# Six prefetch hints and six branches in TensorE's program of a cached attention decode kernel

## The chip, the cores and the metric

The kernel runs on one core of one Trainium2 chip. The metric is the device time of one execution in microseconds (us). Three runs of the kernel before gave 1265.35 to 1266.34 us, with a median of 1266.06 us. Differences of about 0.2% (2.5 us) are taken as what a measurement of this kernel can tell from no change.

Five engines work side by side, each with its own program: TensorE (PE in the profile, with its weight loads as PEld), VectorE (DVE), ScalarE (ACT), GpSimd (POOL) and SyncE (SP). SP issues nearly all the transfers from device memory. Engines wait for each other through semaphores.

## The reference

What is computed is one decode step: a gated sum of an attention block over a long cache and a small token-mixing MLP.

```python
Hq, Hkv, Sk, Dh = 16, 8, 65536, 256            # D = 448, one token
q = (x @ wq).reshape(1, 1, 16, 256)            # two query heads share one KV head
scores = einsum("bhqd,bhkd->bhqk", q, k) * Dh**-0.5
o = einsum("bhqk,bhkd->bhqd", softmax(scores), v)
a = o.reshape(1, 1, 4096) @ wo
b = token_mlp(layernorm(x))                    # w1, b1, gelu, w2, b2 over a token axis of length 1
g = sigmoid((x * gate_w).sum(-1))
return g * a + (1 - g) * b
```

The K cache and the V cache hold 8 x 65536 x 256 bf16 numbers each, 268 MB apiece. All of it has to be read once.

## The kernel before, in words

**Tiling.** The cache is cut into `NP` = 32 blocks, four for each of the 8 KV heads. A block is 16384 keys, laid out as 128 partitions by `NV` = 128 key rows of 256 numbers: 8.39 MB of K and 8.39 MB of V. `kring` holds one and a half blocks of K, `vbuf` one block of V.

**TensorE's loop (lines 521 to 562).** It runs 33 times over `j`. Pass `j` does three things in order. First come the maxima of the block before (`maxima`, line 384). Then come the keys of block `j` (`keys`, line 375), in eight groups `k` of 16 key rows: `transposes(k)` (line 333) turns 16 tiles of K by matmuls into `kst` (line 348), and `scores(k - 1)` (line 360) multiplies 32 turned tiles by the query (line 369). Groups 0 to 3 read the half of K that is loaded at row `HV` = 64 and up; groups 4 to 7 read the other half, at one of two places, so they stand twice in the program, in an `If` and an `Else` (lines 355 to 358). Group 4 has three more `If`s ahead of it (lines 338 to 340). Last come the values of the block before (`values`, line 404): eight matmuls for the denominators (line 393) and 128 for the values (line 400), in pieces that the `pieces` list cuts (0 to 72, 72 to 96, 96 to 112, 112 to 128). The first piece stands twice as well, since the last pass reads it from `kring`. The last pass ends with `tail` (line 467).

[...] Ahead of the loop stands a head that runs once: it turns `x`, computes the queries (lines 495 to 499, which signal `s_q`), and clears two accumulators.

**The other engines.** VectorE and ScalarE copy the turned K tiles out of `kst` (lines 656 and 796), VectorE finds the maxima and scales the accumulator by the change of the maximum (lines 662 to 685, which signal `s_acc`), ScalarE makes the exponentials (line 783, which signal `sem_exp`).

**The order of the transfers.** SP runs a written-out order (lines 255 to 314; every load of K and V is recorded at line 263). K of block `j` is issued when TensorE has turned groups 0 to 3 of block `j - 1` (line 286, semaphore `sem_tr`). V of block `j - 1` follows when TensorE has finished the values before it (line 274, semaphore `sem_pv`), since `vbuf` is free only then. All loads go through one queue in this order. Blocks 0 to 3 start up differently: the two halves of K of blocks 2 and 3 are issued as separate transfers into whichever part of `kring` is free. Pass 2 (`j == LEAD`) has no values.

## Time and profile before

| What | Value |
|---|---|
| Median of three runs | 1266.06 us (1265.35 to 1266.34) |
| Span of the profiled execution, first to last instruction | 1264.2 us |
| Median less span (start and end around the profile's instructions) | 1.9 us |
| TensorE matmuls busy | 955.4 us, 76% of the span |
| VectorE busy, ScalarE busy | 497.4 us and 544.5 us, 39% and 43% |
| Bytes moved | 544.37 MB in 12054 packets |

How to read it: no time of the profiled execution is given apart from its span, so sums are made on the span and 1.9 us are added. A row of the timeline has a start, a busy time, an engine, a source line, what was written from what, and how often; in brackets stands the idle time of the engine ahead of it and what ended that. "issue" there means that the profile shows nothing that the engine waited for: its sequencer was busy with branches, registers or the fetch of code. A row of waits has the total, the number of times and the longest. A row of a DMA queue has packets, megabytes and a share of the time of 16 DMA engines. A row of windows has the stretch, then the busy time of each engine with its instruction count, the granted TensorE clock, the DMA share and GB/s; DMA packets are counted by their start there, so shares of short stretches go above 1 and below it in turn.

### The profile page before, as it was taken

To read this page: it belongs to the slowest core of one execution; us is meant where nothing else is said; L and a number is where in the kernel's file an instruction comes from. 1 tells how busy PE (TensorE), PEld (TensorE's weight loads), DVE (VectorE), ACT (ScalarE), POOL (GpSimd) and SP (SyncE) were. 2 spreads that over 40 slices of the span, in tenths; PEclk is the share of its full clock that TensorE was granted. 3 is DMA by queue.
4 is the path that set the end of the run, shared out by engine and by line. 5 is a ranking of instruction groups with operands and counts; after the bars stand their busy time and mean duration, and the time that the engine had idled before them with its cause. 6 is when DMAs were issued, how large, how long until landed. Compare 5 with 4: busy or idle time off the path is not lost.

```text
span 1264.2 us, 39788 instructions
## 1 busy us (share of the span) xinstructions
PE 955.4 (76%) x17107; PEld 879.2 (70%) x17107; DVE 497.4 (39%) x1124; ACT 544.5 (43%) x691; POOL 0.9 (0%) x7
## 2 busy tenths in 40 slices
PE   4778887778776787767877768876769867698786
PEld 3677876668766687666876657875668756687674
DVE  3333434443543444444344423342333423334342
ACT  2444543345533455333554334443344533345451
POOL 0000000000000000000000000000000000000000
PEclk9878887898888897888987889887888878888898
DMA  9999999999999999999999999999999999999998
GB/s 412 434 421 426 441 431 435 433 431 433 435 433 435 433 431 431 431 440 433 431 435 422 435 435 442 433 425 435 431 431 435 435 433 431 435 431 431 427 448 355
DMA packets 12054, 544.37 MB, mean 431 GB/s; under 512 B 1417, under 2 KB 1676, under 8 KB 2956
## 3 DMA queue, kind: packets, MB, share of 16 engines
q1 hardware_dynamic: 11954, 544.22, 99.7%
q8 instruction: 7, 0.11, 0.0%
q10 hardware_dynamic: 90, 0.01, 0.0%
q14 instruction: 3, 0.02, 0.0%
HBM read 544.22 MB, written 0.00 MB: 430 GB/s over the span
## 4 chain that ended last, share of the span: by engine, by line
DMA 63%; PE 34%; issue 1%; DVE 1%; SPq 0%; DVEq 0%; ACT 0%
DMA kring<-in_A_k_cache_dram 60%; PE kst L348 25%; PE sps L369 6%; DMA vbuf<-in_A_v_cache_dram 2%; PE acc L400 2%; DMA wo_sb<-in_A_wo_dram 1%; PE acc L450 0%; PE sps L388 0%; PE prj L461 0%; SPq L263 0%; PE acc L393 0%; DVE ktT L656 0%; ACT z_b L801 0%; PE sps L386 0%; DVE mrow L667 0%
## 5 line engine op out<-in xcount | busy, mean ns | idle before, releaser
L348 PE MATMUL kst<-ident,kring 128*128 128x128 f32 x4096 | 555.4, 296 | 200.3 <-DMA kring<-in_A_k_cache_dram 177.1
L348 PEld LDWEIGHTS kst<-ident,kring 128*128 128x128 f32 x4096 | 504.1, 154 | 209.2 <-issue 204.1
L796 ACT ACTIVATE ktT<-kst 128x1024 bf16<-128x1024 bf16 x512 | 499.3, 1022 | 348.8 <-PE kst L348 348.0
L656 DVE COPY ktT<-kst 128x1024 bf16<-128x1024 bf16 x512 | 353.9, 692 | 444.0 <-PE kst L348 418.5
L369 PEld LDWEIGHTS sps<-qcur,ktT 128*128 128x128 bf16 x8192 | 237.8, 96 | 2.8 <-issue 0.3
L369 PE MATMUL sps<-qcur,ktT 128*128 128x2 bf16 x8192 | 236.6, 163 | 0.0
L400 PE MATMUL acc<-vbuf,pT 128*2 128x256 bf16 x4008 | 155.2, 328 | 7.2 <-DMA vbuf<-in_A_v_cache_dram 3.6
L400 PEld LDWEIGHTS acc<-vbuf,pT 128*2 128x2 bf16 x4008 | 109.2, 100 | 44.9 <-issue 6.2
L779 ACT ACTIVATE fade<-mdif 128x2 f32<-128x2 f32 x32 | 6.5, 204 | 297.1 <-DVE mdif L673 297.1
L667 DVE TENSOR_REDUCE mrow<-sps 2x1 f32<-2x128 f32 x32 | 8.9, 279 | 156.5 <-PE sps L386 156.5
L388 PEld LDWEIGHTS sps<-mdiag,mones 2*128 2x128 f32 x64 | 11.0, 214 | 27.9 <-DVE mdiag L669 27.9
L783 ACT ACTIVATE pT<-sps,mneg 128x64 f32 x128 | 30.3, 334 | 0.0
L386 PE MATMUL sps<-ident,mcol 128*2 128x128 f32 x32 | 8.9, 279 | 27.7 <-issue 26.2
L388 PE MATMUL sps<-mdiag,mones 2*128 2x2 f32 x64 | 13.7, 282 | 21.3 <-DVE mdiag L669 21.3
L801 ACT ACTIVATE z_b<-z_b 128x448 bf16<-128x448 bf16 x14 | 8.1, 577 | 48.2 <-DVE z_b L643 48.2
L393 PE MATMUL acc<-pT,ones_sq 128*128 128x32 bf16 x256 | 11.9, 181 | 21.8 <-issue 18.3
L386 PEld LDWEIGHTS sps<-ident,mcol 128*2 128x2 f32 x32 | 2.6, 80 | 36.4 <-issue 28.1
L690 DVE COPY accs<-acc 128x288 f32<-128x288 f32 x8 | 3.7, 457 | 60.9 <-PE acc L400 60.9
L662 DVE TENSOR_REDUCE mcol<-sps 128x2 f32<-128x256 f32 x32 | 13.5, 423 | 35.5 <-PE sps L369 35.5
L393 PEld LDWEIGHTS acc<-pT,ones_sq 128*128 128x128 bf16 x256 | 8.7, 99 | 25.8 <-issue 22.2
L685 DVE TENSOR_SCALAR acc<-acc,fader 128x256 f32<-128x256 f32 x32 | 15.8, 493 | 2.5
L672 DVE TENSOR_SCALAR mneg<-sps 128x2 f32<-128x2 f32 x32 | 5.1, 160 | 16.7 <-PE sps L388 16.7
(108 smaller groups left out, 174.6 us busy)
## 6 DMA issues: line engine op xcount, KB each, us to landing
kring<-in_A_k_cache_dram SPq DMA_DIRECT2D x8, 4096.0 KB, 23.8
kring<-in_A_v_cache_dram SPq DMA_DIRECT2D x1, 4608.0 KB, 27.1
wo_sb<-in_A_wo_dram SPq DMA_DIRECT2D x7, 448.0 KB, 25.7
vbuf<-in_A_wq_dram SPq DMA_DIRECT2D x1, 3072.0 KB, 10.4
vbuf<-in_A_v_cache_dram SPq DMA_DIRECT2D x1, 1536.0 KB, 9.2
vbuf<-in_A_v_cache_dram SPq DMA_DIRECT2D x1, 1024.0 KB, 11.3
vbuf<-in_A_v_cache_dram SPq DMA_DIRECT2D x1, 768.0 KB, 12.7
vbuf<-in_A_wq_dram SPq DMA_DIRECT2D x1, 512.0 KB, 11.2
```

The lines of the kernel that those rows point to most:

```text
L348: ins = pe.transpose(kst[:, b, i * P:(i + 1) * P], kring_f[:, at + NT * (k % DC) + 4 * b + i, :], ident[:, :])
L369: ins = pe.matmul(sps[:, 0, 2 * (NT * k + nt):2 * (NT * k + nt) + 2], ktT[:, par, b, ntl * DH + dj:(ntl + 1) * DH:2], qcur[:, dj, :], star ...
L386: pe.transpose(mxT, mcol[:, :], ident[:, :]).then_inc(s_mT, 1)
L388: pe.matmul(mxB, mones[:, :], mdiag[:, :], start=True, stop=True).then_inc(s_mB, 1)
L393: pe.matmul(acc[:, DENC:SELC], ones_sq[:, :], pT[:, r, :], start=False, stop=(r == BODY - 1), skip_group_check=True)
L400: ins = pe.matmul(acc[o:o + REP, 0:DH], pT[:, r, 2 * nt:2 * nt + 2], buf[:, n, :], start=False, stop=False, skip_group_check=True)
L656: vec.tensor_copy(ktT[:, k % KTB, b, :], kst_b[:, b, :]).then_inc(sem_ev[b], 1)
L662: vec.tensor_reduce(out=mcol[:, :], in_=scores_all.rearrange("p (n hh) -> p hh n", hh=REP), axis=AX.X, op=ALU.max)
L667: vec.tensor_reduce(out=mrow[:, :], in_=mxT, axis=AX.X, op=ALU.max)
L685: vec.tensor_scalar(acc[:, 0:DENC], acc[:, 0:DENC], fader[:, :], None, op0=ALU.mult).then_inc(s_acc, 1)
L783: ins = act.activation(pT[:, bass.ds(p0, DC), hh:2 * NT:REP], scores_all.rearrange("p (a r n hh) -> p a hh r n", a=2, r=DC, hh=REP)[:, hal ...
L796: act.activation(ktT[:, k % KTB, b, :], kst_b[:, b, :], AF.Copy).then_inc(sem_ev[b], 1)
```

## The change

Six times at the head of TensorE's program, ahead of everything else that it does, the change marks a place for a branch hint. Each place names one of six branches further down. [...]

The six branches are new and stand inside the loop. Each compares a register with 1 << 20, which the register never reaches, and goes to the same label whether it is taken or not; that label is the next instruction. So no branch changes what is computed. They stand at the top of a pass (`hop(0)`), ahead of groups 3 and 6 of the keys (`hop(1)`, `hop(2)`), in `values` after the waits and ahead of the denominators (`hop(3)`), after 32 of the first 72 value matmuls (`hop(4)`), and after the first piece (`hop(5)`). For `hop(4)` the first piece in its `If` half is cut in two calls, which issue the same 72 matmuls in the same order.

```diff
+    NHOP = 6
...
             one = ones_sq[0:1, 0:1]
+            hints = [pe.mark_branch_hint_location() for _ in range(NHOP)]
+
+            def hop(i, reg):
+                name = "hop_%d" % i
+                pe.br_lt(reg, 1 << 20, on_true=name, on_false=name).branch_hint(hints[i])
+                nc.switch_bb(name)
...
                 for k in range(1, BODY):
+                    if k % 3 == 0:
+                        hop(k // 3, c0)
                     transposes(k, c0 + k, j, *where)
...
                 pe.wait_ge(sem_exp, pe.snap(v + 1, min_val=2, max_val=NP + 1))
+                hop(3, j)
                 denominators()
                 with pe.If(j < NP):
                     pe.wait_ge(sem_v, pe.snap(v * 16, min_val=16, max_val=16 * NP))
-                    some(0, NRING, vbuf)
+                    some(0, 2 * NT, vbuf)
+                    hop(4, j)
+                    some(2 * NT, NRING, vbuf)
                 with pe.Else():
                     piece_wait(0)
                     some(0, NRING, kring)
+                hop(5, j)
...
                 g = pe.snap(g_reg, min_val=1, max_val=H + 1)
+                hop(0, j)
                 with pe.If(j > LEAD):
```

The hints run once. `hop(0)` runs in all 33 passes, `hop(1)` and `hop(2)` in the 32 passes that have keys, `hop(3)` and `hop(5)` in the 32 passes that have values, and `hop(4)` in 31 of these, all but the last.

## The prediction

> **What bounds the kernel now.** I read the first page from the top: busy time, transfers, queues, and the chain that ended last.

> ```profile
> span 1264.2 us, 39788 instructions
> PE 955.4 (76%) x17107; PEld 879.2 (70%) x17107; DVE 497.4 (39%) x1124; ACT 544.5 (43%) x691; POOL 0.9 (0%) x7
> ...
> q1 hardware_dynamic: 11954, 544.22, 99.7%
> q8 instruction: 7, 0.11, 0.0%
> ...
> DMA 63%; PE 34%; issue 1%; DVE 1%; SPq 0%; DVEq 0%; ACT 0%
> ```

> No compute engine is busy for more than 76% of the span, and queue q1, which carries the cache, is busy for 99.7% of it. So the time is a volume over a rate, plus what lies at the two ends. The chain gives TensorE 34%, but the chain names the last releaser of each wait; it does not ask whether the queue was still full when the next load came. For that I take the busy time by stretches.

> ```profile
> 0.00:3.00 3.00, 0.43 (x5) 0.29 (x5) 1.55 (x10) 0.00 (x0) 0.90 (x7) 1.00 0.35 99
> 3.00:122.00 119.00, 81.13 (x1400) 73.69 (x1401) 40.33 (x90) 46.31 (x57) 0.00 (x0) 0.87 1.00 431
> 122.00:1259.00 1137.00, 871.45 (x15661) 803.61 (x15658) 454.13 (x1021) 497.88 (x634) 0.00 (x0) 0.86 1.00 433
> 1259.00:1264.20 5.20, 2.41 (x44) 1.64 (x44) 1.43 (x6) 0.35 (x1) 0.00 (x0) 0.76 0.27 99
> ```

> The last two numbers of each row are the DMA share and GB/s. From 122 us on the transfers run at 433 GB/s without a gap. The start-up from 3 to 122 us runs at 431 GB/s: 119 x (1 - 431/433) = 0.55 us were lost there. That is all that a change on TensorE could win in the transfers.

> Next, how much the transfers can bear when TensorE is late: the issues with their time to landing, and TensorE's longest wait.

> ```profile
> vbuf<-in_A_v_cache_dram SPq DMA_DIRECT2D x31, 28.1
> kring<-in_A_k_cache_dram SPq DMA_DIRECT2D x28, 27.8
> ...
> PE kst L348 <- DMA kring<-in_A_k_cache_dram: 177.1, 29, 9.7
> ```

> A block of 8.39 MB takes 8390/433 = 19.4 us, yet lands 27.8 or 28.1 us after its issue. It stood in the queue behind another block for some 8.5 us. The first load shows how long a transfer takes to begin:

> ```profile
> 0.74 0.41 SPq L255 DMA_DIRECT2D wo_sb<-in_A_wo_dram  x1
> ```

> It was issued at 0.74 us, and the share of 0.35 over the first 3 us is 1.05 us of full work, so transfers began near 1.95, about 1.2 us after. That leaves some 7 us: in the middle of the run a load may be issued 7 us later before the queue runs dry. TensorE also waits 177.1/29 = 6.1 us per pass for K. A few tenths more per pass disappear in this.

> There is one place without that cover, in the start-up:

> ```profile
> 65.60 0.33 SPq L263 DMA_DIRECT2D vbuf<-in_A_v_cache_dram  x1
> ...
> 116.72 0.33 SPq L263 DMA_DIRECT2D kring<-in_A_k_cache_dram  x1
> ...
> 72.52 6.01 PE L348 MATMUL kst<-ident,kring 128*128 128x128 f32 x32 [6.95 <-DMA kring<-in_A_k_cache_dram]
> ...
> wo_sb<-in_A_wo_dram SPq DMA_DIRECT2D x7, 448.0 KB, 25.7
> vbuf<-in_A_wq_dram SPq DMA_DIRECT2D x1, 3072.0 KB, 10.4
> ...
> vbuf<-in_A_wq_dram SPq DMA_DIRECT2D x1, 512.0 KB, 11.2
> ```

> The load at 116.72 us is the second half of K of block 3. What was issued ahead of it is 4032 KB = 4.13 MB of weights (one load of each of the three rows) and five and a half blocks of 8.39 MB, together 50.3 MB. At 433 GB/s from 1.95 us these end at 118.1, or 118.7 with the 0.55 us lost. Issue at 116.72 plus 1.2 us is 117.9. Here nothing is to spare: what TensorE loses between 72.52 us, where K of block 1 releases it, and 116.72 us may become time of the whole kernel.

> **The change, part by part.** *The hints at the head.* They stand ahead of everything on TensorE, once. What hides them is a wait for a small load:

> ```profile
> PE acc L486 <- DMA b_b<-in_B_b_dram: 8.7, 1, 8.7
> ```

> Six instructions at 0.23 us, the dearest that I find below for a sequencer instruction, are 1.4 us inside 8.7 us. Without that cover they would still only move the queries, whose signal releases V of block 0, queued behind the weights and K of block 0 until 1.95 + 12.5 MB/433 = 30.9 us. Cost 0.

> *What the hints may fetch.* Queue q8 carries seven packets of 16 KB. The queues by window say when: one up to 19 us, six up to 73 us, and after that one small packet of the other code queue only.

> ```profile
> q8 instruction: 1, 0.02, 0.3%
> ...
> q8 instruction: 6, 0.10, 0.7%
> ...
> q1 hardware_dynamic: 10924, 513.48, 99.7%
> q14 instruction: 1, 0.01, 0.0%
> ...
> 48.51 0.55 PE L348 MATMUL kst<-ident,kring 128*128 128x128 f32 x3 [2.17 <-issue]
> 63.10 2.47 PE L400 MATMUL acc<-vbuf,pT 128*2 128x256 bf16 x51 [3.58 <-issue]
> ```

> I take these for TensorE's code, since they fall in its first pass, where TensorE stops in the middle of a run of equal matmuls, for 2.17 and 3.58 us, with nothing to wait for; in the 31 later passes neither packets nor such stops show. So the loop stays in the engine's instruction memory once it is there. If the hints bring the code in early, 5.75 us of stops go. What is late next is K of block 1: TensorE would end the first pass 5.75 us sooner and wait 12.7 us in place of 6.95. V of block 1 would be issued near 60 in place of 65.60 us, into a queue that is full until 1.95 + 29.3 MB/433 = 69.6 us (the weights and three blocks). Nothing gained. The packets take 0.7% of 16 engines over 54 us, 1.0 us of one engine each; moved before the loads begin, all seven give back 7/16 = 0.4 us, and fetched twice they cost as much. I take 0, with -0.55 (the loss of the start-up) and +0.4 as ends.

> *The branches.* No row shows a single branch. Three places bound one. Between the last value matmul of pass 1 and the first tile of pass 2 lie some six branches and ten register instructions. Ahead of group 4 lie four branches. Groups 5 to 7 have an `If` and an `Else` each, group 2 has none:

> ```profile
> 79.17 1.95 PE L348 MATMUL kst<-ident,kring 128*128 128x128 f32 x16
> 81.76 1.94 PE L348 MATMUL kst<-ident,kring 128*128 128x128 f32 x16
> 85.07 1.96 PE L348 MATMUL kst<-ident,kring 128*128 128x128 f32 x16 [0.59 <-issue]
> 87.77 1.97 PE L348 MATMUL kst<-ident,kring 128*128 128x128 f32 x16
> 90.37 1.95 PE L348 MATMUL kst<-ident,kring 128*128 128x128 f32 x16
> 92.96 1.95 PE L348 MATMUL kst<-ident,kring 128*128 128x128 f32 x16
> 100.80 5.49 PE L400 MATMUL acc<-vbuf,pT 128*2 128x256 bf16 x128
> 107.69 3.83 PE L348 MATMUL kst<-ident,kring 128*128 128x128 f32 x32 [1.40 <-issue]
> ```

> The first: 1.40/6 = 0.23 us each, with the register work put on the branches. The second: 0.59/4 = 0.15 us. The third: groups 5 to 6 and 6 to 7 are 2.60 and 2.59 us apart, groups 1 to 2, without a branch, 2.59. So where matmuls are queued ahead a branch costs nothing, because the sequencer runs ahead of the array; the 128 value matmuls, which have several branches among them, also run in one piece. An exposed branch lies between 0 and 0.23 us; I take 0.15, from the second place, the nearest to bare branches.

> `hop(1)` and `hop(2)` stand like groups 5 to 7, `hop(4)` and `hop(5)` inside the value matmuls: 0. `hop(3)` stands behind the waits for the accumulator and the exponentials, with the denominators queued behind it and nothing running: 0.15. `hop(0)` stands at the top of a pass, with the maxima and the keys behind it: 0.15. From 72.52 to 116.72 us run hops 1 to 5 of pass 1 and hops 0 and 1 of pass 2: 2 x 0.15 = **0.3 us**, with 0 and 7 x 0.23 = 1.6 us as ends. In the later passes the same 0.3 us, at most 6 x 0.23 = 1.4, lie inside the 6.1 us of waiting and the 7 us of queue: 0. At the end, `hop(0)`, `hop(3)` and `hop(5)` of the last pass lie ahead of this wait for the last pieces of V:

> ```profile
> 1258.19 0.61 PE L400 MATMUL acc<-vbuf,pT 128*2 128x256 bf16 x16 [1.62 <-DMA vbuf<-in_A_v_cache_dram]
> ```

> 3 x 0.23 = 0.7 us is less than 1.62: 0.

> [...]

> **Sum.** Span 1264.2 + 0.3 = 1264.5 us; with the 1.9 us around it, 1266.4, against the median of 1266.06. That is 0.03%, far under the 0.2% (2.5 us) that a measurement of this kernel can tell from no change. I forecast no change.

> **The rivals.** *The first pass gains (faster, within 0.2%).* The hints bring the code in before the loads begin. For it speak the two stops; against it, that the wait for K hides them. At most 0.55 us: 1265.5.

> *The loop no longer stays resident (slower).* The six branches make the loop longer. Nothing shows how much more code the engine keeps; seven packets are known to fit. If the longer loop, or lines taken up by hints, push it over that edge, all seven are fetched again in each of 32 passes. TensorE's stops, 5.75 us as in the first pass, would still fit in its 6.1 us of waiting. What can't be hidden is the queue: 7 x 1.0 us of one engine in 16 is 0.44 us per pass, 14 us in all if the packets spread evenly, and up to 1.0 x 32 = 32 us if one engine serves the same packet each time: 1280 to 1298. It decides from the first packet that comes back in every pass, one each costing 2 us spread or 32 on one engine. Against it: a few instructions are little beside 0.11 MB.

> [...]

> *A new stop in the first two passes (slower).* If the hints upset the order in which code comes in, or a branch meets code that is not there yet, one or two stops of 2.17 to 3.58 us fall between 72.52 and 116.72 us, once, and are paid in full: 1268.6 to 1273.6, starting from 1266.4.

> *The change does not do what it says:* the hints fetch nothing and the branches vanish. 1266.1, no different.

> **How the numbers follow.** Forecast 0.71 (1265.2 to 1267.7). First pass gains 0.07. Change without effect 0.05. Loop no longer resident 0.10. New stop 0.07. Faster by over 0.2% would need a gain four times what the start-up lost; I keep 0.02 of the first rival for what I have not seen. So faster 0.02, same 0.05 + 0.05 + 0.71 = 0.81, slower 0.17. The range reaches below to the 0.55 us plus the half microsecond by which the three runs spread, 1264.8, and above to one stop of 2.17 us in the start-up with the same spread, 1269.2.

> **What would show it.** Right: q1 at 99.7%, the stretch from 122 to 1259 us at 433 GB/s, the load of 116.72 us at 116.7 to 117.3, no more packets on q8 after 73 us. The hints at work: no stop near 48 and 63 us, V of block 1 issued near 60. Wrong: packets of q8 in every pass; stops of over 2 us between 72 and 117 us; time to landing under 21 us in the middle of the run, which would mean a queue that runs dry.

## The result, and the profile after

| | before | after |
|---|---|---|
| Median | 1265.93 us (1265.35 to 1266.79) | 1269.61 us (1265.39 to 1275.99) |
| Executions | 16 | 16 |
| Executions above 1268 us | 0 | 10 |
| Ratio after to before | | 1.0025, 95% interval 1.0015 to 1.0035 |

The change made the kernel slower by 0.25% by the ratio of the comparison, or 3.7 us between the medians. That is just over the 0.2% that counts as a difference here. The median lies 0.4 us above the upper end of the prediction's range, 1269.2 us; the ratio, put on the prediction's 1266.06 us, gives 1269.2 us, that end itself. The executions are as telling as the median: those of before lie within 1.4 us, those of after within 10.6 us. Four of after's are as fast as before (1265.39 to 1265.88 us) and ten lie above 1268 us. So this is no fixed price per pass. Something happens in some executions and not in others. The profiled execution of after is its longest, 1275.99 us, so its profile shows the loss enlarged. (The ratios here and below leave out executions over 1.5% above the fastest of their kernel: three of `e10_twice`, one of `e3_hops_fit`; medians and ranges hold them all.)

The first page of after, the lines that answer to those of before:

```profile
span 1274.2 us, 39985 instructions
PE 989.1 (78%) x17107; PEld 904.2 (71%) x17107; DVE 496.6 (39%) x1124; ACT 545.7 (43%) x691; POOL 0.9 (0%) x7
...
q1 hardware_dynamic: 11954, 544.22, 99.3%
q8 instruction: 8, 0.13, 0.0%
...
DMA 48%; PE 43%; issue 3%; DVE 3%; DVEq 1%; ACT 0%; SPq 0%
```

The volume is the same and q1's share fell from 99.7% to 99.3%: the queue ran dry. TensorE is busy 33.7 us longer with the same 17107 matmuls, so they ran slower. VectorE, which the change does not touch, now has 3% of the chain of work that ended last, against 1%.

Where was it lost? The same bytes lie ahead of each landing of a block of K in both kernels, so the time from landing to landing tells. A landing is the start of the key matmuls that waited for it. Three stretches, before and then after: up to K of block 4, from block 5 to block 7, and from block 17 to block 19. The columns are stretch, engines, clock, DMA share, GB/s.

```profile
3.00:169.77 166.77, 119.42 (x2089) 109.47 (x2090) 59.83 (x134) 69.76 (x88) 0.00 (x0) 0.88 1.01 433
208.47:287.02 78.55, 58.87 (x1050) 54.14 (x1051) 35.03 (x83) 35.00 (x45) 0.00 (x0) 0.85 1.00 433
676.33:754.87 78.54, 57.35 (x1051) 53.65 (x1051) 30.88 (x67) 34.02 (x44) 0.00 (x0) 0.85 1.00 433
```

```profile
3.00:173.67 170.67, 119.93 (x2089) 109.58 (x2090) 59.77 (x134) 69.71 (x88) 0.00 (x0) 0.87 1.01 428
212.46:293.47 81.01, 67.13 (x1051) 61.34 (x1051) 33.13 (x77) 34.76 (x44) 0.00 (x0) 0.75 0.97 409
683.22:764.71 81.49, 65.97 (x1050) 60.32 (x1051) 33.32 (x76) 34.76 (x44) 0.00 (x0) 0.77 0.99 417
```

The span grew by 10.0 us. Of these 3.9 us (170.67 - 166.77) were lost in the start-up, ahead of K of block 4, 2.5 us between blocks 5 and 7, and 2.9 us between blocks 17 and 19. Most of the rest, 0.5 us, fell between blocks 7 and 9. The loads of blocks 6 and 7 are issued in passes 5 and 6, those of blocks 18 and 19 in passes 17 and 18.

The middle first: the long stretch of the prediction, then the granted clock inside pass 5 (block 5 of K, the second block of the second head).

```profile
122.00:1269.00 1147.00, 907.80 (x15715) 831.61 (x15713) 455.33 (x1023) 501.08 (x636) 0.00 (x0) 0.84 1.00 430
...
220.00:224.00 4.00, 4.00 (x48) 3.94 (x47) 1.38 (x2) 1.85 (x2) 0.00 (x0) 0.50 0.91 393
224.00:228.00 4.00, 4.00 (x49) 3.94 (x48) 1.04 (x2) 2.05 (x2) 0.00 (x0) 0.50 0.91 393
```

The transfers ran at 430 GB/s in place of 433. TensorE ran all of 220 to 228 us, without a gap, at a granted clock of 0.50. In the same pass of before, it was back at full clock by 216 us:

```profile
216.00:220.00 4.00, 4.00 (x70) 3.98 (x69) 2.54 (x4) 2.78 (x3) 0.00 (x0) 1.00 1.06 459
```

Next TensorE's waits, after and then before (total, times, longest):

```profile
PE sps L396 <- issue: 32.6, 30, 2.4
...
PE acc L403 <- issue: 25.5, 30, 1.1
...
PE kst L356 <- DVE ktT L671: 16.9, 9, 5.3
```

```profile
PE sps L386 <- issue: 26.2, 30, 2.1
...
PE acc L393 <- issue: 18.3, 30, 0.9
...
PE kst L348 <- DVE ktT L656: 2.4, 3, 0.8
```

The two exposed branches are visible. `hop(0)` stands ahead of the maxima (L396): (32.6 - 26.2)/30 = 0.21 us more per pass. `hop(3)` stands ahead of the denominators (L403): (25.5 - 18.3)/30 = 0.24 us. The last row is the one to follow. TensorE's key tiles now wait 16.9 us for VectorE's copies out of `kst`, up to 5.3 us at a time, where before they waited 2.4 us in all and never over 0.8. The timeline of pass 5 shows it, before and then after:

```profile
203.00 0.27 PE L386 MATMUL sps<-ident,mcol 128*2 128x128 f32 x1 [0.75 <-issue]
...
208.47 6.30 PE L348 MATMUL kst<-ident,kring 128*128 128x128 f32 x32 [3.94 <-DMA kring<-in_A_k_cache_dram]
...
210.30 0.39 DVE L649 TENSOR_TENSOR gu<-wtmp,z_b 128x448 bf16<-128x448 bf16 x1
...
211.03 1.29 DVE L656 COPY ktT<-kst 128x1024 bf16<-128x1024 bf16 x2 [0.34 <-issue]
...
219.97 0.33 SPq L263 DMA_DIRECT2D kring<-in_A_k_cache_dram  x1
```

```profile
208.88 0.37 PE L396 MATMUL sps<-ident,mcol 128*2 128x128 f32 x1 [0.64 <-issue]
...
212.46 3.67 PE L356 MATMUL kst<-ident,kring 128*128 128x128 f32 x16 [1.97 <-DMA kring<-in_A_k_cache_dram]
...
216.26 0.39 DVE L664 TENSOR_TENSOR gu<-wtmp,z_b 128x448 bf16<-128x448 bf16 x1
216.99 1.29 DVE L671 COPY ktT<-kst 128x1024 bf16<-128x1024 bf16 x2 [0.34 <-issue]
...
217.74 3.68 PE L356 MATMUL kst<-ident,kring 128*128 128x128 f32 x16 [1.60 <-DVE ktT L671]
...
222.11 3.65 PE L356 MATMUL kst<-ident,kring 128*128 128x128 f32 x16
...
226.45 3.65 PE L356 MATMUL kst<-ident,kring 128*128 128x128 f32 x16
...
230.14 0.33 SPq L265 DMA_DIRECT2D kring<-in_A_k_cache_dram  x1
```

Read it in this order. When TensorE has done the maxima, VectorE finishes its own part of them and then runs the MLP's mixer, which ends with `gu`. Only then does it copy turned keys. K of the block lands at its own time. TensorE can turn 16 tiles of it, one group, which fill `kst`; the next group needs VectorE's first copy. In this pass of after, TensorE's granted clock was 0.50 from the landing at 212.46 us to 216.13 us, and the 16 tiles took 3.67 us. A copy took some 0.65 us (1.29/2). So, by these numbers, VectorE must be free within 3.67 - 0.65 = 3.0 us of the landing, or TensorE pauses. Before, its first copy began 211.03 - 208.47 = 2.56 us after the landing: no pause. After, 216.99 - 212.46 = 4.53 us: a pause of 1.60 us. Behind that pause the granted clock was 0.50 in each of three more groups (217.74 to 221.42, 222.11 to 225.76 and 226.45 to 230.10 us): some 3.65 us each, in place of 6.30 - 3.65 = 2.65 for the second group and 1.95 for the two behind it. K of block 6 is issued when these four are done: 230.14 - 212.46 = 17.7 us after the landing, in place of 219.97 - 208.47 = 11.5. The 6.2 us between them are the pause (1.6) and the slow groups (1.0 + 1.7 + 1.7), to two tenths. With that the queue runs dry: K of block 6 lands 41.30 us after K of block 5 (253.76 - 212.46), in place of 39.85 (248.32 - 208.47).

The branches are only a part of what put this pass over the edge. VectorE's first copy begins 4.53 - 2.56 = 1.97 us later against the landing. Of these, 1.24 us come from the pass before, whose first two groups took 6.46 us in after and 5.22 us before (in the second 2 us of them the granted clock was 0.50 and 0.73); the two exposed branches are worth 0.45 us.

So the wait for K of 6.1 us per pass, on which the prediction leaned, was the mean of unequal passes. Ahead of the maxima of passes 5, 9, 13 and 17 stands the extra work with which TensorE closes a head, and the mixer's end comes close to the landing. In passes 9 and 13 of before it already came too late, and TensorE paused for VectorE:

```profile
368.52 1.97 PE L348 MATMUL kst<-ident,kring 128*128 128x128 f32 x16 [0.70 <-DVE ktT L656]
...
524.87 1.97 PE L348 MATMUL kst<-ident,kring 128*128 128x128 f32 x16 [0.84 <-DVE ktT L656]
```

There the granted clock was 1.00 in the groups behind the pause (1.97 us each), and nothing was lost.

The start-up needs a look too, since the prediction had a rival there. The first passes of after:

```profile
48.83 1.88 PE L356 MATMUL kst<-ident,kring 128*128 128x128 f32 x11 [2.75 <-issue]
...
65.84 3.16 PE L410 MATMUL acc<-vbuf,pT 128*2 128x256 bf16 x56 [5.29 <-issue]
...
74.86 6.37 PE L356 MATMUL kst<-ident,kring 128*128 128x128 f32 x32 [5.86 <-issue]
...
119.98 0.33 SPq L265 DMA_DIRECT2D kring<-in_A_k_cache_dram  x1
```

The two stops that I put down to fetched code are still there, and in this execution longer (2.75 and 5.29 us, against 2.17 and 3.58). Pass 1 then begins at 74.86 us in place of 72.52, and what ends the idle time ahead of it is no longer the landing of K but "issue". The load that was issued at 116.72 us goes out at 119.98. So in this one execution the prediction's rival of a new stop in the first two passes did come. That the whole 3.9 us of the start-up are due to it is not shown: e1 and e4 below lost 1.5 and 1.6 us there without it. Nor is it what makes the executions of after late: e1 and e3 below are as late, and there the landing of K, at 72.84 and 72.89 us, still begins pass 1.

### The profile page after: what moved, and what is told of

The parts are those of the page before. It is cut to its first block, busy times and chain, and to the rows that moved or that the text cites. A ratio compares the mean times of both kernels' runs of the same rounds, so it can differ in the third digit from the quotient of the medians.

```text
span 1274.2 us, 39985 instructions
## 1 busy us (share of the span) xinstructions
PE 989.1 (78%) x17107; PEld 904.2 (71%) x17107; DVE 496.6 (39%) x1124; ACT 545.7 (43%) x691; POOL 0.9 (0%) x7
## 3 DMA queue, kind: packets, MB, share of 16 engines
q1 hardware_dynamic: 11954, 544.22, 99.3%
HBM read 544.22 MB, written 0.00 MB: 427 GB/s over the span
## 4 chain that ended last, share of the span: by engine, by line
DMA 48%; PE 43%; issue 3%; DVE 3%; DVEq 1%; ACT 0%; SPq 0%
DMA kring<-in_A_k_cache_dram 45%; PE kst L356 29%; PE sps L377 8%; PE acc L410 4%; DMA vbuf<-in_A_v_cache_dram 2%; DMA wo_sb<-in_A_wo_dram 1%; PE acc L464 0%; DVE ktT L671 0%; PE sps L398 0%; ACT z_b L816 0%; PE acc L403 0%; PE prj L475 0%; PE sps L396 0%; DVE z_b L652 0%; DVE wtmp L650 0%
## 5 line engine op out<-in xcount | busy, mean ns | idle before, releaser
L356 PE MATMUL kst<-ident,kring 128*128 128x128 f32 x4096 | 578.7, 303 | 163.1 <-DMA kring<-in_A_k_cache_dram 117.7
L356 PEld LDWEIGHTS kst<-ident,kring 128*128 128x128 f32 x4096 | 523.0, 158 | 174.4 <-issue 152.2
L410 PE MATMUL acc<-vbuf,pT 128*2 128x256 bf16 x4008 | 162.7, 339 | 6.9 <-issue 5.3
L410 PEld LDWEIGHTS acc<-vbuf,pT 128*2 128x2 bf16 x4008 | 111.8, 103 | 49.7 <-issue 6.3
L396 PE MATMUL sps<-ident,mcol 128*2 128x128 f32 x32 | 9.1, 285 | 34.1 <-issue 32.6
L403 PE MATMUL acc<-pT,ones_sq 128*128 128x32 bf16 x256 | 12.1, 183 | 29.4 <-issue 25.5
L396 PEld LDWEIGHTS sps<-ident,mcol 128*2 128x2 f32 x32 | 2.6, 80 | 43.0 <-issue 41.3
L403 PEld LDWEIGHTS acc<-pT,ones_sq 128*128 128x128 bf16 x256 | 8.8, 100 | 33.6 <-issue 33.6
L398 PEld LDWEIGHTS sps<-mdiag,mones 2*128 2x128 f32 x64 | 11.4, 222 | 28.1 <-DVE mdiag L684 28.1
## 6 DMA issues: line engine op xcount, KB each, us to landing
wo_sb<-in_A_wo_dram SPq DMA_DIRECT2D x7, 448.0 KB, 25.0
vbuf<-in_A_wq_dram SPq DMA_DIRECT2D x1, 3072.0 KB, 10.4
vbuf<-in_A_v_cache_dram SPq DMA_DIRECT2D x1, 768.0 KB, 12.7
vbuf<-in_A_wq_dram SPq DMA_DIRECT2D x1, 512.0 KB, 11.2
```

Of the source, the lines that this page charges most:

```text
L356: ins = pe.transpose(kst[:, b, i * P:(i + 1) * P], kring_f[:, at + NT * (k % DC) + 4 * b + i, :], ident[:, :])
L396: pe.transpose(mxT, mcol[:, :], ident[:, :]).then_inc(s_mT, 1)
L398: pe.matmul(mxB, mones[:, :], mdiag[:, :], start=True, stop=True).then_inc(s_mB, 1)
L403: pe.matmul(acc[:, DENC:SELC], ones_sq[:, :], pT[:, r, :], start=False, stop=(r == BODY - 1), skip_group_check=True)
L410: ins = pe.matmul(acc[o:o + REP, 0:DH], pT[:, r, 2 * nt:2 * nt + 2], buf[:, n, :], start=False, stop=False, skip_group_check=True)
```

## The experiments

The first four runs had three theories. **A**: the longer loop costs code fetches (one more packet on q8). **B**: the branches add up on TensorE's path. **C**: the hints upset the fetching of code. After these four I formed **D**, told above: the exposed branches make the mixer end later against the landing of K, and past an edge the clock stays low and the queue runs dry. The later runs set D against B.

| Run | Median, us (range; n) | Ratio to before, 95% | Above 1268 us |
|---|---|---|---|
| e1_hints_skipped | 1270.12 (1265.55 to 1276.4; 12) | 1.0029, 1.0014 to 1.0043 | 9 |
| e2_grow_only | 1265.9 (1265.46 to 1267.09; 11) | 1.0, 0.9991 to 1.0009 | 0 |
| e3_hops_fit | 1270.02 (1268.71 to 1290.13; 7) | 1.0031, 1.0019 to 1.0043 | 7 |
| e4_before_cut | 1267.14 (1265.53 to 1268.15; 11) | 1.0006, 0.9998 to 1.0015 | 1 |
| e5_hops_no_mixer | 1265.76 (1265.34 to 1267.64; 11) | 1.0002, 0.9994 to 1.0011 | 0 |
| e6_hops_0_3 | 1268.28 (1265.5 to 1277.12; 12) | 1.0035, 1.0014 to 1.0055 | 6 |
| e7_hops_1_2_4_5 | 1265.78 (1265.45 to 1267.17; 11) | 1.0003, 0.9994 to 1.0012 | 0 |
| e8_long_mixer | 1277.36 (1273.71 to 1282.37; 6) | 1.0086, 1.0067 to 1.0106 | 6 |
| e9_hop_0 | 1266.91 (1265.67 to 1273.06; 12) | 1.0016, 1.0006 to 1.0026 | 4 |
| e10_twice | 1272.87 (1266.58 to 1300.65; 10) | 1.0038, 1.0015 to 1.006 | 6 |
| e11_hops_short_mixer | 1265.95 (1265.46 to 1267.58; 11) | 1.0001, 0.9992 to 1.001 | 0 |
| e12_short_mixer | 1265.8 (1265.42 to 1267.13; 11) | 1.0003, 0.9994 to 1.0011 | 0 |

Before, run beside them, had 1265.93 us (e1 to e4) and 1265.7 us (e5 to e8, and e9 to e12), never above 1267.58.

### e1: without the hints

The hints stand behind a condition that is never met; the branches stay.

```diff
-            hints = [pe.mark_branch_hint_location() for _ in range(NHOP)]
+            skip_reg = pe.alloc_register("skip_reg")
+            pe.reg_mov(skip_reg, 0)
+            with pe.If(pe.snap(skip_reg, min_val=0, max_val=NP) > LEAD):
+                hints = [pe.mark_branch_hint_location() for _ in range(NHOP)]
```

> The changed kernel with its six hint instructions put behind a condition that is never met, so that they are in the program but don't run; the six branches stay. Theory A (the longer loop: its last instructions fall into a seventh code packet, which the first pass has to wait for before it can turn back): as the changed kernel, median 1268 to 1271 us, V of block 1 issued near 69 us, pass 1 begun near 74.9 us. Theory B (the branches themselves cost sequencer time in every pass): the same, 1268 to 1271. Theory C (the hints upset the order or the time at which code comes in): back to 1266 us, pass 1 begun at 72.5 us.

1.0029, as slow as after. The hints are not the cause: C falls. Nor does its profiled execution have the new stop of after: V of block 1 is issued at 63.74 us, and pass 1 begins with the landing of K at 72.84 us. Up to K of block 4 it has lost 1.5 us, and between blocks 17 and 19 2.9 us. The same wait is in its profile, with 5.2 us at its longest:

```profile
PE kst L359 <- DVE ktT L674: 10.4, 5, 5.2
```

### e2: a longer loop without branches

To the kernel before, eight semaphore increments at the end of the tail, which runs once but stands in the loop.

```diff
+                for _ in range(8):
+                    pe.sem_inc(s_early, 1)
```

> The kernel before, with eight increments of a semaphore that nobody waits for any more, added at the end of the last pass's tail. They run once, after TensorE's last result, and make the loop eight instructions longer; no hint, no branch. Theory A: 1268 to 1271 us with pass 1 begun near 74.5 us, eight packets on the code queue. Theories B and C: 1266 us, pass 1 begun at 72.5 us.

1.0, and no execution above 1267.09 us. Like after, it fetches eight packets in place of seven (its row of q8 reads the same). So the eighth packet costs nothing: A falls, and with it the rival of a loop that is no longer resident. This run holds something else that matters for D: a pause almost as long as that in after, and harmless.

```profile
526.29 3.46 PE L348 MATMUL kst<-ident,kring 128*128 128x128 f32 x16 [1.54 <-DVE ktT L658]
...
530.38 1.95 PE L348 MATMUL kst<-ident,kring 128*128 128x128 f32 x16
```

The pause is 1.54 us, and the group behind the next took 1.95 us; the granted clock was 0.50 from 525 to 529 us and 0.95 from 529 to 533. The profiled executions of e4, e7 and e9 have such a pause as their longest too, 1.52 or 1.53 us, and none of them runs dry behind it. So a kernel without both exposed branches already comes to the edge in its worst passes.

### e3 and e4: branches in a loop that is shorter than before, and its control

Both leave out the first 16 value matmuls of the last block, which shortens the loop; e3 has all hints and branches, e4 has none.

```diff
                 with pe.Else():
                     piece_wait(0)
-                    some(0, NRING, kring)
+                    some(NT, NRING, kring)
```

> The changed kernel, hints and branches and all, with the loop shortened elsewhere: the first 16 value matmuls of the last pass are left out, which stand in a branch of the code that only the last pass runs, so the output lacks their share. The loop is then shorter than that of the kernel before. Theory A: back to 1265.5 to 1266.5 us, pass 1 begun at 72.5 us, spread of the times under 2 us. Theory B: 1268 to 1271 us as the changed kernel. Theory C: 1268 to 1271 us.

> Control for the run above: the kernel before with the same 16 value matmuls of the last pass left out, no hint, no branch. They lie inside the last pass's wait for V, so all theories expect 1265.3 to 1266.5 us.

e3 gave 1.0031, with seven packets on q8 and all seven executions above 1268 us: the branches are slow in a short loop too. K of block 4 lands only 0.7 us later than before, so this loss is not in the start-up. The timeline of its passes 17 and 18:

```profile
677.00 3.67 PE L356 MATMUL kst<-ident,kring 128*128 128x128 f32 x16 [1.59 <-DMA kring<-in_A_k_cache_dram]
...
682.63 3.68 PE L356 MATMUL kst<-ident,kring 128*128 128x128 f32 x16 [1.96 <-DVE ktT L671]
...
724.24 3.68 PE L356 MATMUL kst<-ident,kring 128*128 128x128 f32 x16 [5.05 <-DVE ktT L671]
```

A pause of 1.96 us, three groups of 3.65 to 3.68 us behind it (the time of a group at the clock of 0.50 in after), and a worse pause in the next pass. In e1 the pause of pass 17 was 2.01 us. Both are longer than the 1.54 us of e2 by about what two exposed branches cost in after, 0.21 + 0.24 = 0.45; but these are single executions, and that of e6, with both branches, has 1.50 us at its longest. K of block 17 lands 0.7 us later than before (677.00 - 676.33), K of block 19 4.1 us (758.97 - 754.87): e3 lost 3.4 us in these two passes.

The control e4 was not neutral: 1267.14 us, where I had expected 1265.3 to 1266.5. Its last value matmuls ran slower:

```profile
1259.77 1.02 PE L400 MATMUL acc<-vbuf,pT 128*2 128x256 bf16 x16 [1.03 <-DMA vbuf<-in_A_v_cache_dram]
```

1.02 us for the 16 that took 0.61 before. Of the 2.2 us by which the span of this execution is longer, 0.6 us lie behind this landing. The other 1.6 us were lost ahead of K of block 4, and no run shows why; the cut does not reach there. e3 stands 2.9 us above its control.

### e5: the branches without the mixer

After, with the mixer left out on VectorE and ScalarE (the MLP's part of the output is not computed). TensorE's program is unchanged.

```diff
-                            mixer(vec.snap(kt_reg, min_val=0, max_val=FT - 1))
+                            vec.sem_inc(s_pb, 1)
```

> The changed kernel without the token mixer's work on VectorE and ScalarE in 14 of the passes (VectorE only signals; TensorE's program is unchanged, its two mixer matmuls multiply zeros), so the output lacks the MLP term. Theory D (half a microsecond of branches per pass makes TensorE ready for the next K block while VectorE still works on the mixer; TensorE then pauses, its clock stays at half for three more groups, the next K load is issued some 7 us late and the queue runs dry): back to 1265.5 to 1266.5 us, no dip of the transfers in the middle of the run. Theory B (the branch time adds up on the path by itself): 1268 to 1271 us as with the mixer.

1.0002, none above 1267.64 us. The idle time ahead of the maxima and the denominators is near that of after (33.8 and 25.4 us); of the wait for VectorE only one is left, in the last block, where no mixer runs:

```profile
PE kst L356 <- DVE ktT L673: 0.8, 1, 0.8
```

So the branches alone, added up over 32 passes, are hidden, as the prediction said: B falls. They become time only against the mixer.

### e6 and e7: the exposed two, and the other four

```diff
 e6: hop(0) and hop(3) stay; hop(1), hop(2), hop(4), hop(5) go
 e7: hop(1), hop(2), hop(4), hop(5) stay; hop(0) and hop(3) go
```

> Only the two branches that stand where nothing is queued ahead on TensorE, at the top of a pass and ahead of the denominators, with their two hints. Theories B and D: nearly all of the effect, median 1268 to 1271 us, and the idle time ahead of lines 386 and 393 of the kernel before up by 0.2 us each. If hidden branches matter as well: 1266 to 1268 us.

> Only the four branches among queued matmuls (ahead of groups 3 and 6, and in the values), with their four hints. Theories B and D: 1265.5 to 1266.5 us, as these cost nothing that is seen. If hidden branches matter: 1267 to 1270 us.

e6 gave 1.0035, six of twelve executions above 1268 us; e7 gave 1.0003 and none. (The profiled execution of e6 took 1267.45 us and that of e9, below, 1266.36 us, so no trace shows the late executions of these kernels.) The waits of e7 have the very numbers of before at the two places:

```profile
PE sps L396 <- issue: 26.2, 30, 2.1
...
PE acc L403 <- issue: 18.3, 30, 0.9
...
PE kst L356 <- DVE ktT L669: 2.7, 3, 1.5
```

Which branches are exposed, and that the four others are free, was right.

### e8: a longer mixer, TensorE as before

The same edge from the other side: before, with the mixer's first VectorE instruction issued six times. In the timeline of before it starts 0.53 us ahead of the next one, so this adds 5 x 0.53 = 2.7 us to each mixer pass.

```diff
-                vec.drain()
-                vec.tensor_scalar(W, hbT[:, :], params[:, bass.ds(kt, 1)], None, op0=ALU.mult)
+                for _ in range(6):
+                    vec.drain()
+                    vec.tensor_scalar(W, hbT[:, :], params[:, bass.ds(kt, 1)], None, op0=ALU.mult)
```

> The kernel before, TensorE's program untouched, with the first instruction of VectorE's mixer issued six times in place of once, about 2.7 us more of VectorE in each of 14 passes. Theory D: slower by 3 us or more (1269 to 1285), with pauses of TensorE for VectorE in the mixer passes and groups of 3.65 us in place of 1.95 after them. Theory B: 1266 us, since VectorE has idle time enough and TensorE's path gains no branch.

1.0086, every execution above 1273 us. TensorE's program has no branch more than before, yet:

```profile
PE kst L348 <- DVE ktT L657: 58.0, 15, 6.9
```

The transfers fall to 427 GB/s over its middle:

```profile
122.00:1272.00 1150.00, 898.25 (x15599) 826.00 (x15601) 476.68 (x1090) 498.87 (x634) 0.00 (x0) 0.84 0.99 427
```

By the landings of K, 16.0 us are lost from block 5 to block 19, nearly all of them ahead of blocks 6 and 7, 10 and 11, 14 and 15, 18 and 19. Their loads are issued in passes 5 and 6, 9 and 10, 13 and 14, 17 and 18: the pass behind the closing of each of the first four heads, and the one after it. These four pairs hold the two of after. Behind the pauses of its mixer passes, 1.70 to 6.87 us, one or two groups took 3.3 us and more. VectorE is busy for 39% of the span of before, far from being the bound; what counts is when it is busy.

### e9 and e10: one exposed branch, and four

e9 is e6 without `hop(3)`; e10 is e6 with each of the two branches twice.

> Only the branch at the top of a pass, with its hint: about 0.22 us per pass in place of 0.45. Theory D has an edge, not a slope: most executions near 1266 us, with a few at 1268 to 1277; median 1265.7 to 1267.5 us. If the lost time grew in proportion to the branch time: 1267 us, with little spread.

> The branch at the top of a pass and the one ahead of the denominators, each twice in a row, with a hint each: about 0.9 us per pass. Theory D: more of the passes that open a head fall into the slow clock, 1270 to 1280 us, with pauses of TensorE for VectorE near passes 5, 9, 13 and 17. In proportion to the branch time: 1270 to 1274 us.

e9: 1.0016, four of twelve above 1268 us. e10: 1.0038, six of ten, with three of them at 1288 to 1301 us, where no other kernel has more than one. One of its waits:

```profile
PE acc L401 <- issue: 32.4, 30, 1.4
```

Two branches ahead of the denominators cost (32.4 - 18.3)/30 = 0.47 us, twice the 0.24 of one. The order e7, e9, e6, e10 is that of the added delay, in the number of late executions of the first three (0 of 11, 4 of 12, 6 of 12) and in the size of the worst. Four and six of twelve are too near each other to tell e9 from e6, and the ratios don't rise in steps that these intervals tell apart; the profiled execution of e10 is a nearly undisturbed one (1267.92 us), with pauses of 1.64 and 1.78 us and groups of 1.97 us right behind them; behind the longer one the granted clock was 1.00 from 685 to 693 us. So a pause of that length did not always leave the clock low.

### e11 and e12: a shorter mixer, with and without the branches

The mixer does the same with two VectorE instructions of eleven fewer: a multiplication and an addition become one instruction, and a scaling moves into ScalarE's tanh (a small copy also moves up by one instruction).

```diff
-                vec.tensor_scalar(W, hbT[:, :], params[:, bass.ds(kt, 1)], None, op0=ALU.mult)
-                vec.drain()
-                vec.tensor_scalar(U, W, params[:, bass.ds(kt + FT, 1)], None, op0=ALU.add)
+                vec.tensor_scalar(U, hbT[:, :], params[:, bass.ds(kt, 1)], params[:, bass.ds(kt + FT, 1)],
+                                  op0=ALU.mult, op1=ALU.add)
...
-                vec.tensor_scalar(Z, Z, GC0, None, op0=ALU.mult).then_inc(s_u, 1)
...
-                        act.activation(z_b[:, :], z_b[:, :], AF.Tanh).then_inc(s_tanh, 1)
+                        act.activation(z_b[:, :], z_b[:, :], AF.Tanh, scale=GC0).then_inc(s_tanh, 1)
```

> The changed kernel with all hints and branches and a shorter mixer on VectorE: a multiply and an add made one instruction, and one scaling moved into the activation on ScalarE, so that two of its eleven instructions fall away (rounding between them changes a little). That takes about 1 us off the time at which VectorE is ready to copy K tiles. Theory D: back to 1265.5 to 1266.5 us although all branches run. Theory B: 1268 to 1271 us.

> The kernel before with the same shorter mixer, no hint, no branch. The transfers were full from 122 us on, so there is at most the 0.55 us of the start-up to win, which the mixer doesn't touch: 1265.3 to 1266 us under all theories.

With all hints and branches of the change in place, e11 gives 1.0001 and no execution above 1267.58 us: the loss is gone. Its waits keep the branches' price, and the wait for VectorE is that of before:

```profile
PE acc L403 <- issue: 25.6, 30, 1.1
...
PE kst L356 <- DVE ktT L669: 2.3, 3, 1.1
```

e12, the short mixer without branches, gives 1.0003. It lowers the wait to 0.7 us, but there is nothing to win: the queue was full already. No version here beats the kernel before.

## Why the prediction was right or wrong

**The bound: right.** The kernel is bound by its transfers, and nothing was to be won beyond 0.55 us. The kernels that lost nothing, e2, e5, e7, e11 and e12, have medians of 1265.76 to 1265.95 us, though TensorE's program differs among them.

**The hints: right.** e1 shows that they neither help nor harm (1.0029 without them, 1.0025 with them); what such a hint does inside the chip no run here shows. Nothing comes early with them: the two stops of the first pass are still there. The stops differ from execution to execution; the second is 5.29 us in after, 2.98 in e1, where the hints don't run, 1.76 in e3.

**Which branches are exposed: right; their price: low.** e7 against e6 (1.0003 against 1.0035) shows that hops 1, 2, 4 and 5 cost nothing, and hops 0 and 3 alone the loss. I took 0.15 us each, with 0.23 as the upper end. They measure 0.21 and 0.24 in after. Ahead of the denominators it is 0.24 in every kernel with that branch; ahead of the maxima it differs: in e6 it is (37.9 - 26.2)/30 = 0.39, and e9 with this branch alone gives (35.9 - 26.2)/30 = 0.32:

```profile
PE sps L394 <- issue: 35.9, 30, 2.4
```

With 0.23 each the start-up term would have been 0.46 in place of 0.3 us, no other forecast. The start-up varies more than that without any branch: K of block 4 lands 0.1 us earlier than before in e12 and 1.6 us later in e4.

**The later passes at nothing: wrong, and this is the step that failed.** I wrote that 0.3 us, at most 1.4, "lie inside the 6.1 us of waiting and the 7 us of queue". The 6.1 us hold on average, and e5 shows that the branches are hidden where nothing else is in the way. Three things were missed. The 6.1 us is a mean over 29 passes, and the waits of passes 5, 9 and 13, each behind the closing of a head, are 3.94, 3.13 and 2.72 us. And the wait for K is not idle time of the kernel: VectorE runs the mixer in it, and has to be done 3.0 us after the landing by the sum above (3.67 - 0.65). The margin of pass 5 in the profiled execution of before was 3.0 - 2.56 = 0.4 us, and two exposed branches cost 0.45; passes 9 and 13 had no margin left. The stall that follows is not of their size: a pause and three groups at a clock of 0.50 cost 6.2 us at once in after. And the 7 us of queue were too many. In pass 9 of e3 K was issued 14.96 us after the landing, 3.7 us later than in before (11.26), and nothing was lost; in pass 5 of after it was 6.2 us later, and 1.5 us were lost. So, by these two passes, the queue bore more than 3.7 us and less than 6.2.

That the ratio meets the upper end of the range is luck. I had set that end for one stop of 2.17 us in the start-up, not for a loss in the later passes.

That the two exposed branches carry the loss is shown by e6 and e7, that they do it against the mixer by e5 and e11, and that a late mixer is enough by e8. That slow groups (3.65 to 3.68 us at a clock of 0.50 in after, 3.65 to 3.68 in e1 and e3, 3.3 and more in e8) and the late load are the way from the pause to the lost time is seen in these four traces. Why only some passes of some executions go over the edge I read from how the clock falls in the passes; that part is argued, not shown. The same 128 value matmuls took 3.67 us in one pass of the kernel before and 5.08 in another:

```profile
193.79 5.08 PE L400 MATMUL acc<-vbuf,pT 128*2 128x256 bf16 x128
...
661.69 3.67 PE L400 MATMUL acc<-vbuf,pT 128*2 128x256 bf16 x128
```

The granted clock was 0.71 in the first stretch and 1.00 in the second. So with the clock these value matmuls ended 5.08 - 3.67 = 1.4 us earlier or later against their start. The margin of 0.4 us is that of one pass in one execution; the branches, as I read it, shift the whole spread of margins by 0.45 us.

**The rivals.** The loop stayed resident: no packet of q8 came after 78 us in after, and e2 and e3 bear it out. A new stop in the first two passes, 1268.6 to 1273.6 us, holds the measured median, but not for its reason. It did come in the profiled execution of after, where 3.9 of the 10.0 us were lost in the start-up. But e3 lost only 0.7 us there and is as slow, and e5 and e11, with all hints and branches and eight packets, have none above 1267.64 us in 22 executions. I did not have the rival that happened: a wait on VectorE that takes the place of the wait for K. Its row stood in the profile of before, 2.4 us in three waits, and I passed over it for its size. Such a row is not a cost yet, but a sign: two of the three waits, those of passes 9 and 13, say that the margin was already used up there. (The third is in the last block, where no mixer runs; e5 has it too.)

**What stays open.** No run isolates why the clock was still 0.50 behind a pause in after, and why not always: pauses of 1.60 to 2.01 us were followed by three groups of 3.65 to 3.68 us in after, e1 and e3, those of 1.64 and 1.78 us in e10 by none, that of 1.77 us in pass 7 of after by one (3.57 us), and that of 0.60 us in pass 9 of e3 by two (3.67 and 3.65 us). I took away what causes the pause (e5, e11), not what holds the clock. Where the later dry places of a single execution fall can therefore not be foretold.

## What to carry to other kernels

A mean wait per pass is no cover: look for the pass with the shortest wait, and ask what other engines do during that wait and how late they may end. A small row of waits of a critical engine on one that is "only 39% busy" marks an edge, and a few tenths of a microsecond past it can cost several: in pass 5 of after 0.45 us of branches stood beside a pause of 1.60 us, three groups at a clock of 0.50, a load issued 6.2 us later and 1.5 us lost. Where executions spread from the old time upwards after an edit that should cost a fixed amount, look for such an edge, and take the pressure from its other side (here VectorE's mixer) to test it.

## What the runs showed of the hardware

One exposed branch on TensorE, compare included, cost 0.21 (after) to 0.39 us (e6) until the next matmul, and two in a row ahead of the denominators 0.47 us (e10). The four in streams of queued matmuls left the waits at 26.2 and 18.3 us, as before, and the ratio at 1.0003 (e7).
